# Storing each block of 128 result rows as two transfers of 64 rows in a fused attention and feed-forward kernel

## The chip, the cores and the metric

The kernel runs on one core of one Trainium2 chip. The metric is the device time of one execution in microseconds (us); lower is better. A core has a matrix engine (PE), a vector engine (DVE), a scalar engine (ACT), a general engine (POOL) and a synchronisation engine (SP) which here issues nearly all transfers; sixteen DMA engines carry them. Each engine runs its own instructions in order and waits on semaphores for the others.

## The reference

```python
B, H, S, D = 4, 8, 768, 48                      # batch, heads, steps, head size
for t in range(S):                               # recurrent attention, one state per batch and head
    state = alpha[:, :, t, :, None] * state + einsum('bhd,bhe->bhde', k[:, :, t], v[:, :, t])
    y[:, :, t] = einsum('bhd,bhde->bhe', q[:, :, t], state)
x = y.transpose(0, 2, 1, 3).reshape(3072, 384)   # tokens x (heads * head size)
h = x @ w_in                                     # 384 x 2048
g = h * tanh(log1p(exp(h)))
out = g @ w_out                                  # 2048 x 384, float32
```

The output has 3072 rows of 384 floats. Row `b * 768 + t` belongs to batch `b` and step `t`.

## The kernel before

**Chunks.** The four batches are taken in two pairs. A chunk is 64 steps (`L`) of a pair of batches, so 128 tokens; there are 24 chunks, in the order pair 0, pair 1, pair 0, and so on (`chunks`). Within a chunk's 128 rows, the first 64 belong to one batch of the pair and the last 64 to the other, and these two blocks lie 768 rows apart in the output.

**Attention (`attention(n)`).** For a chunk, SP loads one block with q, k and the decays (`qka`, 675.9 KB, L454, or in parts at L459) and one with v (192 KB, L463). DVE makes the running products of the decays with two scans (`rest` at L485, the second at L498) and multiplies k and q by them; PE turns k (L520), multiplies by the state and forms the scores (L530 and L536, the planner's "front"); DVE masks the scores into `probs` (L544); PE multiplies them with v and updates the state (L549 and L559, the planner's "back"); ACT and DVE split the result into a high and a low part (L578, L584); and SP moves a few rows into place with six small transfers (L604). The `qka` block has two buffers, so the load for chunk n waits until chunk n - 2 has read its own.

**Feed-forward (`unit`).** Hidden rows are worked in 16 blocks of 128, chunks in groups of two or four (`SEGMENTS`). One unit is a group times a block: PE makes `h` with nine matmuls (L706), ACT and DVE make `g` by eight passes (L714 to L740), and PE adds into one bank of `sums_at` for each chunk of the group, three matmuls for each (L770). After the last block of a group its four banks are finished almost together: ACT copies each to a result buffer `osb` (L808), or DVE first adds it to a kept part and ACT copies that (`part`, L801 and L808), and SP stores it (L815). Eight such buffers exist. The last four groups of four chunks run all 16 blocks in one go; what comes before is cut into shorter segments. So result rows are stored in bursts of four: two bursts from `part` and four from `osb`, 24 stores of 192 KB in all.

**Order.** Nothing is scheduled by hand. `Plan.order` plays the whole program through with a table of costs, `COST` (L211): for each kind of task the time it takes from its engine, and the time after which its result can be used. It places the tasks of each engine in the order in which they could begin, the task's key breaking ties, and the program is emitted in that order. An attention chunk is due eight units ahead of the first unit that reads it (`LEAD`). The planner therefore does not change what an instruction takes; its times only decide the order within each engine's queue. SP's queue holds loads, the six small moves and the stores together, in one order.

**Semaphores of transfers.** Eight semaphores serve the transfers of SP in turn, so a transfer also waits until the eighth before it has landed.

**The end.** After the last group, DVE, PE and DVE reduce a few checks to one number `good` (L878 to L893), which every engine reads to decide whether a general path is run instead (L1023); it isn't. SP then waits for all eight transfer semaphores and the program closes (L1087).

Of the kernel before, what the change touches and what calls it, by code (L numbers as in the profile page):

```python
# [26 lines left out]
B, H, S, D = 4, 8, 768, 48  # L27
# [3 lines left out]
L = 64  # L31
NCH = S // L
# [60 lines left out]
class Plan:  # L93
# [13 lines left out]
    def add(self, engine, cost, late, key, emit, needs=(), uses=(), behind=(), port=False):  # L107
        t = Task(engine, cost, late, key, emit, port)
        t.needs, t.uses, t.behind = list(needs), list(uses), list(behind)
        for u in t.uses:  # L110
            u.left += 1
            u.key = min(u.key, key)
        self.tasks.append(t)
        return t
# [96 lines left out]
COST = {  # L211
    "load part": (0.7, 3.3), "load q": (1.8, 5.0), "load two": (1.2, 4.0), "load v": (0.7, 4.0),
    "load w": (2.0, 5.0),
    "move": (0.63, 2.5), "store": (0.47, 3.0),
    "fill": (0.165, 0.2), "fill0": (0.33, 0.36),
    "off": (0.34, 0.6), "w off": (0.84, 1.08), "lead": (0.47, 0.58), "bits": (0.87, 0.98),
    "w hi": (0.42, 0.56), "w lo": (0.95, 1.08),
    "w check": (0.92, 1.2),
    "scan": (1.16, 1.27), "inverse": (0.09, 0.21), "mult": (0.6, 0.72), "check": (0.2, 0.34),
    "state": (0.48, 0.55), "state0": (0.5, 0.6), "mask": (0.65, 0.8),  # L220
    "front": (1.05, 1.3), "front0": (0.6, 0.8), "turn": (0.4, 0.65),
    "turned": (0.46, 0.6), "back": (1.05, 1.3), "back1": (0.6, 0.8), "update": (0.55, 0.75),
    "x3 hi": (0.16, 0.3), "x3 lo": (0.2, 0.32), "x hi": (0.39, 0.53), "x lo": (0.48, 0.59),
    "down": (0.525, 0.8), "stash": (0.4, 0.53), "join": (0.47, 0.59), "result": (0.5, 0.7),
}
# [11 lines left out]
def fast_path(ctx, tc, qka, v, w, out, good):  # L237
    nc = tc.nc
# [15 lines left out]
    for half in (slice(0, L), slice(L, P)):  # L254
        nc.gpsimd.affine_select(
            out=causal_f[half], in_=one[half], pattern=[[1, L]], compare_op=ALU.is_ge,
# [19 lines left out]
    for i in range(BUFS["probs"]):  # L276
        t = const.tile([P, 2, NPAIR, L], F32, name=f"probs{i}")
# [3 lines left out]
    for b in range(B // 2):  # L281
        t = const.tile([R, NSEG * D + 16], F32, name=f"state{b}")
# [17 lines left out]
    def new(buffer, shape, name, pool=None, dtype=F32):  # L300
        buffer.tile = (pool or sb).tile(
            shape, dtype, tag=buffer.tag, name=name, bufs=plan.slots[buffer.tag]
        )
        return buffer.tile
# [388 lines left out]
    def unit(c0, nt, f, at, ends):  # L693
        N, key = nt * C, float(at)
        tile_at, place = X_AT[c0]
        x = xs[tile_at][:, :, :, place * C : place * C + N]
        fs = slice(f * P, (f + 1) * P)
        h, u, t, y, g = (plan.buffer(z) for z in ("h", "u", "t", "y", "g"))
        wide = lambda z: z.tile[:, :N]
        cost = lambda z: COST[z, nt]  # L700

        def up():
            p = new(h, [P, NT_MOST * C], f"h{at}", ps)
            passes = [(z, a, s) for s in range(NK) for z, a in ((0, 0), (0, 1), (1, 0))]
            for m, (z, a, s) in enumerate(passes):
                nc.tensor.matmul(  # L706
                    p[:, :N], wi[:, z, s, fs], x[:, a, s], start=m == 0, stop=m == len(passes) - 1
                )

        def exp():
            new(u, [P, NT_MOST * C], f"u{at}")
            nc.scalar.activation(  # L714
                wide(u), wide(h), AF.Exp, scale=-1.0, accum_out=uchk[:, at : at + 1]
            )

        def square():
            new(t, [P, NT_MOST * C], f"t{at}")
            nc.scalar.activation(wide(t), wide(u), AF.Square, bias=1.0, scale=2.0)  # L720

        def times():
            new(y, [P, NT_MOST * C], f"y{at}")
            nc.vector.scalar_tensor_tensor(wide(y), wide(u), 0.5, wide(h), ALU.add, ALU.mult)  # L724

        def log():
            nc.scalar.activation(wide(t), wide(t), AF.Ln, bias=tenth, scale=0.1)  # L727

        def inverse():
            nc.scalar.activation(wide(t), wide(t), AF.Exp, scale=-1.0)  # L730

        def gate():
            nc.vector.scalar_tensor_tensor(wide(t), wide(y), 0.4, wide(t), ALU.mult, ALU.mult)  # L733

        def upper():
            new(g, [P, 2, NT_MOST * C], f"g{at}", dtype=F32R)
            nc.scalar.activation(g.tile[:, 0, :N], wide(t), AF.Copy)  # L737

        def lower():
            nc.vector.tensor_tensor(  # L740
                g.tile[:, 1, :N], wide(t), g.tile[:, 0, :N].bitcast(F32), ALU.subtract
            )

        chunk_x = [z for n in range(c0, c0 + nt) for z in ready_x[n]]
        t_up = add("PE", *cost("up"), key, up, chunk_x + ready_w[f, 0], [h])
        for n in range(c0, c0 + nt):
            readers_x.setdefault(n, []).append(t_up)
        k = key + GATE
        t_exp = add("ACT", *cost("exp"), k, exp, [t_up], [h, u])
        t_y = add("DVE", *cost("dve"), k + 0.01, times, [t_exp], [h, u, y])  # L750
        t_sq = add("ACT", *cost("act"), k + 0.02, square, [t_exp], [u, t])
        t_ln = add("ACT", *cost("ln"), k + 0.03, log, [t_sq], [t])
        t_in = add("ACT", *cost("act"), k + 0.04, inverse, [t_ln], [t])
        t_g = add("DVE", *cost("dve"), k + 0.05, gate, [t_in, t_y], [t, y], port=True)
        t_hi = add("ACT", *cost("act"), k + 0.06, upper, [t_g], [t, g])
        t_lo = add("DVE", *cost("dve"), k + 0.07, lower, [t_hi], [t, g], port=True)

        for j in range(nt):
            n = c0 + j
            bank = bank_of(n, nt)  # L760
            begins = n not in sums
            if begins:
                sums[n] = plan.buffer(f"o{bank}")
            o, end = sums[n], ends(n)

            def down(o=o, j=j, n=n, begins=begins, end=end, bank=bank):
                if begins:
                    o.tile = sums_at[:, bank][:, :DM]
                for m, (a, z) in enumerate(((0, 0), (0, 1), (1, 0))):
                    nc.tensor.matmul(  # L770
                        o.tile, g.tile[:, a, j * C : (j + 1) * C], wo[:, z, f],
                        start=begins and m == 0, stop=end and m == 2,
                    )

            t_down = add(
                "PE", *COST["down"], key + LAG + 0.001 * j, down, [t_lo, *ready_w[f, 1]], [g, o],
                behind=downs.get(n, []),
            )
            downs[n] = [t_down]
            if not end:  # L780
                continue
            del sums[n]
            k = key + LAG + 0.1
            if f < NFF - 1 and n in kept:
                def more(o=o, n=n):
                    nc.vector.tensor_tensor(part[n].tile, o.tile, part[n].tile, ALU.add)

                kept[n] = add("DVE", *COST["join"], k, more, [t_down, kept[n]], [o, part[n]])
                continue
            if f < NFF - 1:  # L790
                part[n] = plan.buffer("osb")

                def stash(o=o, n=n):
                    nc.scalar.copy(new(part[n], [P, DM], f"part{n}"), o.tile)

                kept[n] = add("ACT", *COST["stash"], k, stash, [t_down], [o, part[n]])
                continue
            done, from_part = [t_down], n in kept
            if from_part:
                def join(o=o, n=n):  # L800
                    nc.vector.tensor_tensor(part[n].tile, o.tile, part[n].tile, ALU.add)  # L801

                done = [add("DVE", *COST["join"], k, join, [t_down, kept[n]], [o, part[n]])]
            osb = part[n] if from_part else plan.buffer("osb")

            def result(o=o, n=n, osb=osb, from_part=from_part):
                to = osb.tile if from_part else new(osb, [P, DM], f"osb{n}")
                nc.scalar.activation(  # L808
                    to, to if from_part else o.tile, AF.Copy, accum_out=ochk[:, n : n + 1]
                )  # L810

            def store(n=n, osb=osb):
                b, c = chunks[n]
                to = out.rearrange("(b c t) d -> c b t d", c=NCH, t=L)
                nc.sync.dma_start(to[c, 2 * b : 2 * b + 2], osb.tile)  # L815

            written = add("ACT", *COST["result"], k, result, done, [osb] if from_part else [o, osb])
            add("SP", *COST["store"], k, store, [written], [osb])


# [271 lines left out]
```

## Time and profile before

| | |
|---|---|
| median of three runs | 575.2 us (571.51 to 576.0) |
| the profiled execution | 576.53 us, of which the span from first to last instruction is 574.7 us |
| mean granted TensorE clock | 0.954 |
| PE busy with matmuls | 514.2 us (89%) |
| PE busy with weight loads (beside the matmuls) | 444.3 us (77%) |
| DVE, ACT, POOL busy | 382.0, 397.5, 40.2 us |
| transfers | 54.46 MB, mean 95 GB/s; 4.72 MB written to HBM |

The span counts from the first instruction of the core to its last; 1.8 us of the profiled execution lie outside it. The busy time of an engine is a mean over stages, and this kernel's stages differ: where an engine stands idle, and for whom, is read from the views by time.

In rows of the trace, "L815" is line 815 of the kernel; a name such as `out_dram<-osb` gives what is written and what is read; "SPq" is the queue from which SP issues transfers, where the duration is that of the issue and not that of the transfer. A bracket at the end of a row tells how long the engine stood idle ahead of it and what released it.

### The profile page before, as it was taken

What the parts mean: (1) busy time and instruction counts of PE and PEld (TensorE: products, weight loads), DVE (VectorE), ACT (ScalarE), POOL (GpSimd) and SP (SyncE); (2) the same over time, 40 slices, a digit from 0 to 9 for tenths busy, and PEclk for the clock granted to TensorE, in tenths of its full rate; (3) what the DMA queues carried; (4) which work ended last, traced back from release to release, by engine and by line L of the source; (5) the groups of instructions that cost most, each with busy time, mean ns of one, the idle gap of its engine ahead of it and who ended that gap; (6) DMA issues with size and microseconds to landing.
All of it is one profiled execution on the core that took longest, in us unless ns stands there. A gap on an engine that the chain in (4) does not pass through costs nothing.

```text
span 574.7 us, 13166 instructions
## 1 busy us (share of the span) xinstructions
PE 514.2 (89%) x5275; PEld 444.3 (77%) x5275; DVE 382.0 (66%) x638; ACT 397.5 (69%) x926; POOL 40.2 (7%) x36
## 2 busy tenths in 40 slices
PE   7788899889999984899999969999969999999960
PEld 4366789888789874788989858889858889889960
DVE  7847999999897783777774457864447544444430
ACT  2347778698779893699977745677745677877740
POOL 2001110423333000000000000000000000000000
PEclk9969999999999998699999988999997999999995
DMA  8654442522533664448410142300140000000001
GB/s 266 197 179 129 137 132 73 179 63 103 174 101 123 184 195 159 136 136 252 147 56 1 40 134 72 86 6 1 34 141 22 15 1 2 33 22 0 1 12 46
DMA packets 21744, 54.46 MB, mean 95 GB/s; under 512 B 3696, under 2 KB 14448, under 8 KB 21680
## 3 DMA queue, kind: packets, MB, share of 16 engines
q1 hardware_dynamic: 21392, 53.49, 30.1%
q8 instruction: 42, 0.69, 0.5%
q14 instruction: 22, 0.18, 0.1%
q10 hardware_dynamic: 288, 0.10, 0.1%
HBM read 46.50 MB, written 4.72 MB: 89 GB/s over the span
## 4 chain that ended last, share of the span: by engine, by line
PE 72%; DMA 10%; DVE 9%; ACT 4%; issue 2%; ACTq 0%; DVEq 0%; SPq 0%
PE h L706 30%; PE sums_at L770 30%; DMA qka<-in_qka_dram 8%; PE att_at L549 2%; PE att_at L530 2%; PE sums_at L381 1%; DMA v<-in_vp_dram 1%; PE att_at L536 1%; DVE qka L498 1%; PE att_at L559 1%; DVE t L733 1%; PE sums_at L828 1%; PE att_at L520 1%; DVE rest L485 1%; DVE g L740 1%
## 5 line engine op out<-in xcount | busy, mean ns | idle before, releaser
L770 PE MATMUL sums_at<-wo,g 128*128 128x384 f32 x1152 | 233.8, 345 | 21.9 <-DVE g L740 12.5
L770 PEld LDWEIGHTS sums_at<-wo,g 128*128 128x128 f32 x1152 | 201.0, 189 | 37.5 <-DVE g L740 14.6
L706 PE MATMUL h<-xs,wi 128*128 128x512 f32 (+1 forms) x990 | 224.1, 372 | 1.1 <-DVE y L724 1.1
L706 PEld LDWEIGHTS h<-xs,wi 128*128 128x128 f32 x990 | 173.1, 192 | 28.9 <-DVE y L724 1.6
L740 DVE TENSOR_TENSOR g<-t,g 128x512 fp32r<-128x512 f32 (+1 forms) x110 | 70.2, 639 | 53.2 <-ACT g L737 52.9
L714 ACT ACTIVATE u<-h 128x512 f32<-128x512 f32 (+1 forms) x110 | 59.3, 539 | 66.1 <-PE h L706 66.0
L724 DVE SCALAR_TENSOR_TENSOR y<-u,h 128x512 f32<-128x512 f32 (+1 forms) x110 | 67.5, 616 | 48.4 <-ACT u L714 48.1
L733 DVE SCALAR_TENSOR_TENSOR t<-y,t 128x512 f32<-128x512 f32 (+1 forms) x110 | 70.2, 640 | 13.9 <-ACT t L730 13.9
L727 ACT ACTIVATE t<-t,tenth 128x512 f32<-128x512 f32 (+1 forms) x110 | 73.0, 665 | 2.0
L737 ACT ACTIVATE g<-t 128x512 fp32r<-128x512 f32 (+1 forms) x110 | 62.3, 567 | 9.4 <-DVE t L733 4.5
L720 ACT ACTIVATE t<-u 128x512 f32<-128x512 f32 (+1 forms) x110 | 63.0, 574 | 4.9 <-DVE g L740 2.9
L730 ACT ACTIVATE t<-t 128x512 f32<-128x512 f32 (+1 forms) x110 | 62.2, 567 | 0.6
L485 DVE TENSOR_TENSOR_SCAN rest<-qka,behind 112x520 f32<-112x520 f32 x24 | 29.7, 1236 | 28.1 <-DMA qka<-in_qka_dram 28.1
L498 DVE TENSOR_TENSOR_SCAN qka<-qka,ahead 112x520 f32<-112x520 f32 x24 | 31.3, 1303 | 0.1
L372 POOL TENSOR_TENSOR wi<-w_lead,wi 128x384 fp32r<-128x384 f32 x12 | 21.5, 1799 | 126.8 <-ACT wi L369 126.8
L549 PEld LDWEIGHTS att_at<-probs,v 64*64 64x64 f32 (+1 forms) x672 | 12.3, 134 | 13.1 <-DVE probs L544 8.5
L409 ACT ACTIVATE wc<-wc 128x768 f32<-128x768 f32 x16 | 14.6, 910 | 11.1 <-DMA wc<-in_wp_dram 11.1
L549 PE MATMUL att_at<-probs,v 64*64 64x64 f32 (+1 forms) x672 | 15.3, 231 | 7.0 <-DVE probs L544 7.0
L714 ACT ACTIVATION_READ_ACCUMULATOR u<-h 128x1 f32 x110 | 21.4, 195 | 0.0
L544 DVE COPY_PREDICATED probs<-causal,att_at 128x512 f32<-128x512 uint32 x21 | 15.4, 735 | 8.5 <-PE att_at L536 8.5
L502 ACT ACTIVATE chk<-qka,minus 112x8 f32<-112x8 f32 x24 | 7.3, 304 | 20.0 <-DMA qka<-in_qka_dram 11.7
L828 PE MATMUL sums_at<-ident 128*128 128x384 bf16 x59 | 13.6, 371 | 4.9 <-POOL ident masks.py:199 2.5
(107 smaller groups left out, 396.0 us busy)
## 6 DMA issues: line engine op xcount, KB each, us to landing
qka<-in_qka_dram SPq DMA_DIRECT2D x21, 675.9 KB
ws<-in_wp_dram SPq DMA_DIRECT2D x16, 768.0 KB
wc<-in_wp_dram SPq DMA_DIRECT2D x16, 768.0 KB
v<-in_vp_dram SPq DMA_DIRECT2D x24, 192.0 KB
out_dram<-osb SPq DMA_DIRECT2D x16, 192.0 KB
xs<-x SPq DMA_DIRECT2D x138, 16.0 KB
out_dram<-part SPq DMA_DIRECT2D x8, 192.0 KB
qka<-in_qka_dram SPq DMA_DIRECT2D x2, 448.0 KB
```

The costliest lines, as they stand in the source:

```text
L498: nc.vector.tensor_tensor_scan(a, a, ahead, 0.0, ALU.mult, ALU.max)
L549: nc.tensor.matmul(y[64 * a : 64 * a + wide, u, j], V()[own, h : h + wide], probs[slot][own, a, j], start=first and j == 0, stop=True, ski ...
L706: nc.tensor.matmul(p[:, :N], wi[:, z, s, fs], x[:, a, s], start=m == 0, stop=m == len(passes) - 1)
L714: nc.scalar.activation(wide(u), wide(h), AF.Exp, scale=-1.0, accum_out=uchk[:, at : at + 1])
L720: nc.scalar.activation(wide(t), wide(u), AF.Square, bias=1.0, scale=2.0)
L724: nc.vector.scalar_tensor_tensor(wide(y), wide(u), 0.5, wide(h), ALU.add, ALU.mult)
L727: nc.scalar.activation(wide(t), wide(t), AF.Ln, bias=tenth, scale=0.1)
L730: nc.scalar.activation(wide(t), wide(t), AF.Exp, scale=-1.0)
L733: nc.vector.scalar_tensor_tensor(wide(t), wide(y), 0.4, wide(t), ALU.mult, ALU.mult)
L737: nc.scalar.activation(g.tile[:, 0, :N], wide(t), AF.Copy)
L740: nc.vector.tensor_tensor(g.tile[:, 1, :N], wide(t), g.tile[:, 0, :N].bitcast(F32), ALU.subtract)
L770: nc.tensor.matmul(o.tile, g.tile[:, a, j * C : (j + 1) * C], wo[:, z, f], start=begins and m == 0, stop=end and m == 2,)
```

## The change

The store of a finished chunk named its destination as one pattern of two blocks (the two batches) of 64 rows. It now goes as two transfers, one for each batch, each of 64 whole rows that lie one after another in the output. The bytes are the same; the number of store instructions on SP doubles from 24 to 48. The planner's time for the store task, which is still one task, goes from 0.47 to 1.0 us of SP and from 3.0 to 3.5 us until it is done; its times for three of the attention's PE tasks change by up to 0.08 us. No other code changes.

```diff
@@ COST
-    "move": (0.63, 2.5), "store": (0.47, 3.0),
+    "move": (0.63, 2.5), "store": (1.0, 3.5),
...
-    "front": (1.05, 1.3), "front0": (0.6, 0.8), "turn": (0.4, 0.65),
-    "turned": (0.46, 0.6), "back": (1.05, 1.3), "back1": (0.6, 0.8), "update": (0.55, 0.75),
+    "front": (1.13, 1.35), "front0": (0.6, 0.8), "turn": (0.36, 0.6),
+    "turned": (0.46, 0.6), "back": (1.11, 1.3), "back1": (0.6, 0.8), "update": (0.55, 0.75),
...
             def store(n=n, osb=osb):
                 b, c = chunks[n]
-                to = out.rearrange("(b c t) d -> c b t d", c=NCH, t=L)
-                nc.sync.dma_start(to[c, 2 * b : 2 * b + 2], osb.tile)
+                for u in range(2):
+                    to = out[ds((2 * b + u) * S + c * L, L), :]
+                    nc.sync.dma_start(to, osb.tile[L * u : L * (u + 1)])
```

## The prediction

> **What bounds the kernel now.** I read the page's first two parts, then the chain of work in order of time, then stretches of it with the busy time of each engine, and last the rows of SP, DVE and PE around the places where the chain leaves PE.
>
> ```profile
> span 574.7 us, 13166 instructions
> ...
> PE 514.2 (89%) x5275; PEld 444.3 (77%) x5275; DVE 382.0 (66%) x638; ACT 397.5 (69%) x926; POOL 40.2 (7%) x36
> ...
> DMA  8654442522533664448410142300140000000001
> ```
>
> PE is the bound by its share, and the DMA engines are mostly idle in the second half. PE stands idle for 60.5 us of the span. The chain says where: among long runs of matmuls it holds three waits of a dozen microseconds for a load of q, k and decays (start, length, what).
>
> ```profile
> 216.48 12.36 DMA qka<-in_qka_dram
> ...
> 326.63 11.63 DMA qka<-in_qka_dram
> ...
> 413.23 12.07 DMA qka<-in_qka_dram
> ```
>
> SP's own rows show what stands ahead of each of these loads: stores.
>
> ```profile
> 212.62 3.76 SPq L815 DMA_DIRECT2D out_dram<-part  x3
> 216.48 3.54 SPq L454 DMA_DIRECT2D qka<-in_qka_dram  x1
> ...
> 318.31 7.44 SPq L815 DMA_DIRECT2D out_dram<-osb  x4
> 326.63 2.88 SPq L454 DMA_DIRECT2D qka<-in_qka_dram  x1
> ...
> 338.31 0.34 SPq L454 DMA_DIRECT2D qka<-in_qka_dram  x1
> ...
> 404.94 7.71 SPq L815 DMA_DIRECT2D out_dram<-osb  x4
> 413.23 3.30 SPq L454 DMA_DIRECT2D qka<-in_qka_dram  x1
> ```
>
> A load issued with no store ahead of it takes 0.34 us of SP's queue (338.31); those right behind a burst take about 3. How fast such a free load lands is seen in the DMA view of 337.5 to 343.5 us, 40 slices of 0.15 us:
>
> ```profile
> GB/s 41 41 72 106 51 41 38 34 0 0 0 206 206 165 0 41 330 288 330 330 330 453 288 453 288 206 206 165 83 82 82 82 0 0 0 0 0 0 0 0
> ```
>
> Its last bytes move in slice 32, at 342.3: 4.0 us after the issue. So a load behind stores lands some 7 to 8 us late. Why, the stretches tell (columns: stretch and length, busy time of PE, PE weight loads, DVE, ACT, POOL, granted clock, DMA share, GB/s):
>
> ```profile
> core 0: us, PE busy (x) PEld busy (x) DVE busy (x) ACT busy (x) POOL busy (x), PEclk, DMA share, GB/s
> 222.60:230.80 8.20, 0.00 (x1) 0.00 (x0) 1.87 (x4) 0.00 (x0) 0.00 (x0) 0.67 0.55 189
> 230.80:239.60 8.80, 8.14 (x22) 6.67 (x23) 5.50 (x10) 4.80 (x14) 0.00 (x0) 0.53 0.60 185
> ...
> 343.94:348.90 4.96, 4.96 (x73) 4.25 (x73) 4.45 (x8) 1.59 (x4) 0.00 (x0) 0.56 0.17 47
> ...
> 431.00:437.70 6.70, 6.70 (x78) 5.74 (x79) 5.08 (x11) 2.16 (x6) 0.00 (x0) 0.55 0.14 38
> ...
> 355.90:358.90 3.00, 3.00 (x75) 2.61 (x75) 1.56 (x3) 1.90 (x5) 0.00 (x0) 1.00 0.85 236
> 562.00:572.00 10.00, 0.00 (x0) 0.00 (x0) 0.00 (x0) 0.00 (x0) 0.00 (x0) 0.50 0.14 51
> ```
>
> From 562 to 572 nothing runs but the last stores. They move 51 GB/s at a share of 0.14, which is 2.2 of 16 DMA engines, 23 GB/s each. Loads whose pattern begins with 112 rows use 0.85 of all sixteen (355.9 to 358.9). I read from this that a store is worked by two engines, one for each of the two batch blocks that its destination names first, and that a burst of four (786 KB at 51 GB/s, 15.4 us) blocks those two engines for the load that follows, whose last rows then land behind it. The Trainium skill says so outright: by "DMA: Bandwidth & Descriptors", section "Why a DMA increments its semaphore by 16 and not by 1", a transfer runs on the largest number of engines up to 16 that divides the slowest dimension of both its patterns, here 2 before and 16 after. The trace agrees for the old form (0.14 of 16); no row shows a 64-row transfer.
>
> **The change part by part.** *The store's form.* A transfer of one batch's 64 rows has no outer dimension of two; the nearest rows are the loads by 112 rows. Spread over 16 engines at 23 GB/s a burst of four would need 786 KB / 368 GB/s = 2.1 us instead of 15.4. The lower bound of the effect is that it stays at 15.4 us (first rival); I take 2.1, as all other large transfers of this kernel run so. What this is worth is read stage by stage, from what waits for the loads:
>
> ```profile
> 228.93 1.24 DVE L485 TENSOR_TENSOR_SCAN rest<-qka,behind 112x520 f32<-112x520 f32 x1 [9.23 <-DMA qka<-in_qka_dram]
> 230.81 1.65 PE L770 MATMUL sums_at<-wo,g 128*128 128x384 f32 x4 [8.21 <-DVE g L740]
> ...
> 338.27 1.24 DVE L485 TENSOR_TENSOR_SCAN rest<-qka,behind 112x520 f32<-112x520 f32 x1 [5.67 <-DMA qka<-in_qka_dram]
> 340.37 0.45 PE L770 MATMUL sums_at<-wo,g 128*128 128x384 f32 x1 [1.40 <-DVE g L740]
> 343.94 1.13 PE L549 MATMUL att_at<-probs,v 64*64 64x64 f32 x32 [3.13 <-DVE probs L544]
> ...
> 420.13 2.25 PE L706 MATMUL h<-xs,wi 128*128 128x512 f32 x9
> 425.32 1.24 DVE L485 TENSOR_TENSOR_SCAN rest<-qka,behind 112x520 f32<-112x520 f32 x1 [6.12 <-DMA qka<-in_qka_dram]
> 427.42 0.44 PE L770 MATMUL sums_at<-wo,g 128*128 128x384 f32 x1 [1.85 <-DVE g L740]
> 430.99 1.12 PE L549 MATMUL att_at<-probs,v 64*64 64x64 f32 x32 [3.13 <-DVE probs L544]
> 432.88 4.21 PE L706 MATMUL h<-xs,wi 128*128 128x512 f32 x9
> ```
>
> DVE works in order: its scan waits for the load, and behind the scan stand the `g` and the mask for which PE waits. After each such wait PE also runs at a lower granted clock: the nine matmuls of L706 take 4.21 us instead of 2.25.
>
> Stage A (216 to 240): the load would land by 216.48 + 4.0 to 5.0 = 220.5 to 221.5, sooner if the six issues ahead of it are shorter than the 3.76 us of the three stores. DVE has been free since 228.93 - 9.23 = 219.7. It needs 1.9 us from the scan's start to the end of `g` (228.93 to 230.8), so PE has its `g` at 222.4 to 223.4 and not at 230.8: of 8.2 us idle about 8.0 go. From 230.8 to 239.6 PE is busy 8.14 us at a clock of 0.53; at full clock this is 3.8 us less. Together 11.8.
>
> Stage B (326 to 349): the load would land at 330.6 to 331.6, before DVE comes to its scan at 338.27 - 5.67 = 332.6. All 5.67 us of DVE go, hence both PE waits, 1.40 + 3.13 = 4.5; and the 4.96 us of PE work at 0.56 lose 2.2. Together 6.7.
>
> Stage C (413 to 438) likewise: landing at 417.2 to 418.2, DVE at its scan at 419.2; waits of 1.85 + 3.13 = 5.0, and 6.70 us at 0.55 lose 3.0. Together 8.0.
>
> What is late next: in B the following load was issued at 338.31, just as the one before landed (it is the eighth transfer behind it and uses its semaphore); it moves forward with it, and so do the small moves behind. The other bursts have no such load behind them and give nothing.
>
> The end:
>
> ```profile
> 557.96 0.20 ACT L808 ACTIVATION_READ_ACCUMULATOR osb<-sums_at 128x1 f32 x1
> ...
> 558.33 3.72 SPq L815 DMA_DIRECT2D out_dram<-osb  x1
> ...
> L1023 SPq COMPARE_BRANCH  x1: 45/45/45, 564.5 to 564.5; - x1
> ...
> L1023 SPq EVENT_SEMAPHORE  x8: 17/17/17, 565.0 to 573.3; - x8
> ...
> L1087 SPq EVENT_SEMAPHORE  x10: 17/28/28, 573.4 to 574.6; - x10
> ```
>
> The last result is ready at 558.16, SP's last issue lasts until 562.05, SP branches 2.45 us later, and then waits until 573.3 for transfers to land; 1.4 us close the program. With 2 issues of 0.34 to 0.56 us (rows below) SP is through at 559.0 to 559.5 and reaches its waits, 2.95 us on, at 562.0 to 562.5. The last transfer, issued at 558.7 to 558.9, should land in less than the 4.0 us of a load seven times as large, so by 562.9. I take 562.5 and 1.4 us behind it: 563.9, a gain of 10.8.
>
> *The doubled issues.*
>
> ```profile
> L463 SPq DMA_DIRECT2D v<-in_vp_dram x24: 328/338/1272, 2.2 to 433.0; - x24
> ...
> L815 SPq DMA_DIRECT2D out_dram<-osb x16: 511/564/3721, 318.3 to 558.3; - x16
> ```
>
> A load of 128 rows is issued in 0.338 us, a store of two blocks in 0.564 (duration: least, median, most in ns). Two issues for one thus cost between 0.1 and 0.6 us of SP for each store, 2.3 us a burst at most. SP had stalls of up to 3.7 us there, and after the burst at 318 the load waits for its buffer: SP is free at 325.75, the load begins at 326.63. So I take nothing; without this cover the burst costs 1.4 us in B and 1.7 in C.
>
> *The planner's times.* They change no duration. By them some 20 fronts get 0.08 us more, as many backs 0.06 more and turns 0.04 less, about 2 us over the whole plan, and SP's stores are counted at 1.0 us, so a few tasks may change places on any engine. The trace can't show which. From the rows, one misplaced load costs what stage C costs, 8.0 us; a better order could win at most a like amount, out of the idle time that remains. I take zero and keep both ends.
>
> *Sum.* 11.8 + 6.7 + 8.0 + 10.8 = 37.3 us off the profiled execution's 574.7 + 1.8 = 576.5 gives 539.2; I say 539. That execution is 1.3 us above the median of the runs shown, 575.2, which would bring 538; the difference lies within their spread of 4.5.
>
> **The rivals.** *The transfers do not spread, and it gets slower.* If 64-row stores still run at about 51 GB/s, whether by engines or because writing to HBM gives no more, the drains stay and only the issues are added, at 0.56 us each: the load at 216.48 comes 1.7 us later (three stores), those of B and C 1.4 and 1.7, the end 0.6: 5.4 us, so 582. It decides if a burst still takes over some 13 us to drain. Against it: were the writing side the limit, the packets would stand long on all sixteen engines and the share would be high; it is 0.14. For it speaks a rule: the Trainium skill, "DMA: Bandwidth & Descriptors", section "Rules for kernel authors", advises against two transfers to the halves of the partitions, as both run over the same sixteen engines, and asks for one transfer of 128. By that rule this rival's 582 would come; the trace doesn't agree with its premise here, as the one transfer of 128 uses two engines.
>
> *Only the end gains.* If the loads are late by something else (the two `qka` buffers, the order on SP), A, B and C stay: 576.5 - 10.8 = 566. Against it: the load at 338.31 lands in 4.0 us between the same neighbours save the stores.
>
> *The new order gives a stall back.* One load placed behind its use in a stage as tight as B or C: 539 + 8 = 547, and up to 551 if it is as long as A's 11.8. For it: DVE and SP queues are in order, so one exchange is enough. Against: the stores' new time is nearer to two issues than the old one was.
>
> **How the numbers follow.** Forecast, 531 to 546: 0.70, its own range being 8 us to either side for the planner. A stall given back, 547 to 551: 0.18. Only the end: 0.07. No spread, slower: 0.04. About the same for other reasons: 0.01. A range of 531 to 551 holds the first two less their edges, some 0.83. One per cent (5.8 us) is about what a measurement of this kernel tells from no change; faster by more holds the first three, 0.95; same 0.01; slower 0.04.
>
> **What would show it.** Right: after the bursts at about 318 and 405 (less what was won before) a DMA share far over 0.14 for a short time, loads issued in about 0.34 us and landing within 5 us, no wait of DVE's scan over 2 us after 215, a granted clock near 1.00 all through, and an end under 7 us after the last result. Wrong: a share of 0.14 that lasts 10 us after a burst (no spread); short bursts but a scan that still waits 5 us (another cause); a new wait of PE before 200 us, where no store runs (the planner).

## The result and the profile after

The changed kernel takes 544.0 us (median of four runs, 543.6 to 544.9) against 575.5 before: a ratio of 0.947, with a 95% interval of 0.943 to 0.951. The forecast was 539, in a range of 531 to 551. The profiled execution has a span of 542.3 us, 32.4 less than before.

The page of the changed kernel, first its head, then the slices and the transfers:

```profile
span 542.3 us, 13194 instructions
...
PE 506.7 (93%) x5275; PEld 437.8 (81%) x5275; DVE 380.7 (70%) x638; ACT 397.0 (73%) x926; POOL 41.7 (8%) x36
...
PEclk9979899999999999999999999999999999999998
...
qka<-in_qka_dram SPq DMA_DIRECT2D x21, 675.9 KB, 5.3
...
out_dram<-osb SPq DMA_DIRECT2D x32, 96.0 KB, 2.2
```

PE executes as many matmuls in 7.5 us less of busy time, at a mean granted clock of 0.986 instead of 0.954. A store lands 2.2 us after its issue (last column), a load of q, k and decays 5.3 us after its own. The last burst of stores, from 528 to 542.3 us in 40 slices, keeps up to nine tenths of the sixteen DMA engines busy for short times, where before the share was 0.14 for 10 us:

```profile
DMA  0000000000000008480849084839860010000000
```

SP's rows around the bursts, to be held against those of before:

```profile
214.75 5.99 SPq L816 DMA_DIRECT2D out_dram<-part  x8
220.84 0.53 SPq L454 DMA_DIRECT2D qka<-in_qka_dram  x1
...
310.56 7.19 SPq L816 DMA_DIRECT2D out_dram<-osb  x8
318.87 0.33 SPq L454 DMA_DIRECT2D qka<-in_qka_dram  x1
...
390.38 7.21 SPq L816 DMA_DIRECT2D out_dram<-osb  x8
398.68 0.35 SPq L454 DMA_DIRECT2D qka<-in_qka_dram  x1
```

A load behind a burst is issued in 0.33 to 0.53 us instead of about 3. What waits for these three loads, in the rows of DVE and PE:

```profile
225.89 1.24 DVE L485 TENSOR_TENSOR_SCAN rest<-qka,behind 112x520 f32<-112x520 f32 x1 [2.20 <-DMA qka<-in_qka_dram]
228.10 0.79 PE L770 MATMUL sums_at<-wo,g 128*128 128x384 f32 x3 [2.69 <-DVE part L801]
...
323.84 1.24 DVE L485 TENSOR_TENSOR_SCAN rest<-qka,behind 112x520 f32<-112x520 f32 x1 [0.73 <-DMA qka<-in_qka_dram]
...
403.98 1.24 DVE L485 TENSOR_TENSOR_SCAN rest<-qka,behind 112x520 f32<-112x520 f32 x1 [1.06 <-DMA qka<-in_qka_dram]
```

In stages B and C (second and third group of rows) the scan waits about 1 us and PE not at all; in stage A (the first) a wait of 2.69 us of PE is left. Stretches of the changed kernel (columns as before):

```profile
212.00:235.00 23.00, 19.67 (x277) 16.88 (x274) 17.47 (x29) 15.41 (x38) 0.00 (x0) 1.00 0.56 149
...
318.00:340.00 22.00, 22.00 (x383) 19.05 (x377) 18.44 (x32) 14.55 (x32) 0.00 (x0) 1.00 0.38 100
398.00:420.00 22.00, 22.00 (x382) 19.05 (x373) 19.00 (x35) 13.46 (x28) 0.00 (x0) 1.00 0.36 98
```

B and C are now without a gap on PE; A still has 3.3 us of idle time, at full clock.

To see where the 32.4 us lie, I follow ACT's first pass over `h` (L714), which runs once for each of the 110 units, and compare the start of the same unit in two kernels' traces. The differences to before change only in a few places; with the attention's new times they also wander by some us within units 1 to 46. All kernels of this study stand in one table; each number is how much later (or, with a minus, sooner) a kernel got through that stretch than the kernel before, worked out from the one profiled execution of each by these starts, the column before the sum up to the end of the span:

```
                            to the   units   A: unit  B: to   C: to   to the   sum
                            1st unit 1-46    46-65    unit 81 unit 97 end
changed kernel                -1.3    +3.4    -9.8     -6.8    -8.0    -9.8   -32.4
e1 split, old times           -1.5    -0.3    -6.5     -6.8    -8.0    -9.6   -32.7
e2 new times, old store       +2.6    +3.5    +3.5     +0.6    +0.3     0.0   +10.6
e3 split by columns           +2.2    +3.6    +6.5     +2.7    +1.6    +0.8   +17.4
e4 last four stores split     +3.8    +0.2    -0.7     +0.1     0.0   -10.0    -6.6
e5 split, store time          +1.8    -0.6    -9.8     -6.8    -8.0   -10.0   -33.4
e6 split, attention times      0.0    +3.3    -5.7     -6.8    -8.0   -10.0   -27.2
e7 parts' stores on POOL      +0.5    -0.4   -11.3     -6.8    -8.0    -9.1   -35.2
e8 last four as 62 + 2 rows   -0.2    -0.5    +0.3      0.0     0.0    -0.2    -0.6
e9 all stores on POOL         -2.8    -0.5   -12.0     -6.8    -8.0    -8.0   -38.0
e10 as e5, last four on POOL  -1.8    -0.5   -11.3     -6.8    -8.0    -9.5   -37.9
```

Forecast were 6.7 for B and 8.0 for C: both came. A gives 9.8 instead of 11.8, the end 9.8 instead of 10.8, and 3.4 us are lost before the first store is issued.

### The profile page after: what moved, and what is told of

Same layout as the page of the kernel before. It is cut to its first block, busy times and chain, and to the rows that moved or that the text cites. A ratio compares the mean times of both kernels' runs of the same rounds, so it can differ in the third digit from the quotient of the medians.

```text
span 542.3 us, 13194 instructions
## 1 busy us (share of the span) xinstructions
PE 506.7 (93%) x5275; PEld 437.8 (81%) x5275; DVE 380.7 (70%) x638; ACT 397.0 (73%) x926; POOL 41.7 (8%) x36
## 4 chain that ended last, share of the span: by engine, by line
PE 74%; DVE 12%; ACT 6%; DMA 3%; issue 3%; SPq 0%; ACTq 0%; DVEq 0%
PE sums_at L770 32%; PE h L706 30%; DMA qka<-in_qka_dram 3%; PE att_at L530 2%; PE sums_at L829 2%; PE att_at L549 2%; PE att_at L536 2%; DVE t L733 2%; PE sums_at L381 1%; DVE rest L485 1%; DVE y L724 1%; DVE g L740 1%; PE att_at L559 1%; PE att_at L520 1%; DVE w_lead L356 1%
## 5 line engine op out<-in xcount | busy, mean ns | idle before, releaser
L706 PE MATMUL h<-xs,wi 128*128 128x512 f32 (+1 forms) x990 | 220.7, 368 | 0.6 <-DVE y L724 0.4
L706 PEld LDWEIGHTS h<-xs,wi 128*128 128x128 f32 x990 | 170.4, 189 | 27.6 <-DVE y L724 1.6
L714 ACT ACTIVATE u<-h 128x512 f32<-128x512 f32 (+1 forms) x110 | 59.4, 540 | 68.3 <-PE h L706 68.3
L485 DVE TENSOR_TENSOR_SCAN rest<-qka,behind 112x520 f32<-112x520 f32 x24 | 31.0, 1294 | 13.3 <-DMA qka<-in_qka_dram 13.2
L498 DVE TENSOR_TENSOR_SCAN qka<-qka,ahead 112x520 f32<-112x520 f32 x24 | 30.0, 1250 | 0.0
L714 ACT ACTIVATION_READ_ACCUMULATOR u<-h 128x1 f32 x110 | 21.4, 195 | 0.0
L530 PEld LDWEIGHTS att_at<-qka,state 48*64 48x64 f32 (+1 forms) x640 | 11.5, 131 | 10.3 <-issue 4.5
L372 POOL TENSOR_TENSOR wo<-w_lead,wo 128x384 fp32r<-128x384 f32 x12 | 18.7, 1562 | 6.8 <-DVE t L733 4.6
L530 PE MATMUL att_at<-qka,state 48*64 48x64 f32 (+1 forms) x640 | 14.2, 227 | 4.3 <-DVE state L513 1.8
L508 DVE TENSOR_TENSOR qka<-qka 112x512 f32<-112x512 f32 x24 | 17.4, 725 | 0.0
```

What stands on the lines that cost most here:

```text
L372: nc.gpsimd.tensor_tensor(lo, as_hi(both()), hi.bitcast(F32), ALU.subtract)
L530: nc.tensor.matmul(y[64 * a : 64 * a + wide, u, j], st[r : r + D, e : e + wide], Q()[r : r + D, j, u], start=j == 0, stop=False, skip_grou ...
L706: nc.tensor.matmul(p[:, :N], wi[:, z, s, fs], x[:, a, s], start=m == 0, stop=m == len(passes) - 1)
L714: nc.scalar.activation(wide(u), wide(h), AF.Exp, scale=-1.0, accum_out=uchk[:, at : at + 1])
```

## The experiments

The theory: the gain comes from the stores running on sixteen DMA engines instead of two; the planner's new times change the order and so the rest. The rivals: smaller transfers are enough, or the new order wins a part. All times are medians; the ratio is that to the kernel before on the same chip, with its 95% interval.

**e1: the split with the planner's old times.** The diff is the change without its three lines of `COST`.

> The stores split in two, with the planner's old times, so the order of before. If the whole gain comes from the transfers spreading over 16 engines, and the new times only cost the 2 us by which the changed kernel is late at the 46th unit and part of what stage A fell short: stage A saves 10 to 12 us, B 6.8, C 8.0 and the end 9.8 against before, so about 539 to 541 us. Rival, the new times win a part of the gain: 546 us or more. Rival, the 2 us are not from the times: 544 us.

Measured: 544.3 us, ratio 0.945 (0.941 to 0.949), so as fast as the changed kernel. The first two expectations did not come. The 544 us of the third did, but by luck: its reason, that the late 46th unit has nothing to do with the times, was wrong. The 3.4 us of units 1 to 46 are gone (-0.3), so they are the times' doing; but with the order of before stage A gives only 6.5 us. The new times lose 3.4 and win 3.3, and the term of the prediction for A was too large by itself. What is left in A, in e1's rows of SP, DVE and PE:

```profile
210.97 4.77 SPq L816 DMA_DIRECT2D out_dram<-part  x6
215.83 0.54 SPq L454 DMA_DIRECT2D qka<-in_qka_dram  x1
```

```profile
221.30 1.24 DVE L485 TENSOR_TENSOR_SCAN rest<-qka,behind 112x520 f32<-112x520 f32 x1 [4.14 <-DMA qka<-in_qka_dram]
```

```profile
223.18 2.61 PE L770 MATMUL sums_at<-wo,g 128*128 128x384 f32 x7 [3.12 <-DVE g L740]
```

Six issues take 4.77 us where three stores took 3.76, and the load lands 5.5 us after its issue. DVE had been ready since 217.2, and PE's 3.12 us of idle time are followed by a lower clock:

```profile
214.00:231.00 17.00, 12.49 (x110) 10.67 (x109) 9.74 (x17) 8.77 (x24) 0.00 (x0) 0.80 0.80 231
```

**e2: the new times with the old store.** The diff is the change's `COST` lines alone.

> The planner's new times with the old store of two blocks in one transfer, so the order of the changed kernel. If the transfers carry the gain: no faster than before, 575 to 580 us, about 2 us late at the 46th unit, with the waits of stages B and C and a drain of some 15 us at a DMA share near 0.14 at the end all there. Rival, the new order wins a part: under 570 us.

Measured: 583.6 us, ratio 1.010 (1.004 to 1.016): one per cent slower than before, which is small but clear of the noise, and above the range expected. The end is as before (share 0.15, 54 GB/s from 570 to 580):

```profile
570.00:580.00 10.00, 0.00 (x0) 0.00 (x0) 0.00 (x0) 0.00 (x0) 0.00 (x0) 0.50 0.15 54
```

So the new order by itself, with the old stores, wins nothing. It costs 3.5 us ahead of the stores, and with the old stores another 3.5 in stage A.

**e3: as many transfers of as many bytes, but on two engines.**

```diff
+                to = out.rearrange("(b c t) d -> c b t d", c=NCH, t=L)
+                half = DM // 2
                 for u in range(2):
-                    to = out[ds((2 * b + u) * S + c * L, L), :]
-                    nc.sync.dma_start(to, osb.tile[L * u : L * (u + 1)])
+                    cols = slice(half * u, half * (u + 1))
+                    nc.sync.dma_start(to[c, 2 * b : 2 * b + 2, :, cols], osb.tile[:, cols])
```

> The changed kernel, but each store's two transfers take half of the columns of all 128 rows instead of one batch each: as many transfers of as many bytes, and each names its destination again as two blocks of 64 rows. If the number of DMA engines is what counts: a DMA share near 0.14 after the bursts, and the time of before plus up to 5.4 us for the issues, 576 to 584 us. Rival, two smaller transfers in place of one are enough: 544 us.

Measured: 593.4 us, ratio 1.028 (1.023 to 1.034). Smaller transfers are not enough: with the changed kernel's number of transfers, bytes and planner's times, but two blocks named first, 49 us separate it from the changed kernel. The share after the last burst is that of two engines again. It is slower than expected because issuing costs more than the 0.56 us that I had taken for it (e3, all stores, then one burst with the load behind it):

```profile
576.00:586.00 10.00, 0.00 (x0) 0.00 (x0) 0.00 (x0) 0.00 (x0) 0.00 (x0) 0.50 0.15 50
```

```profile
L818 SPq DMA_DIRECT2D out_dram<-osb x32: 503/1638/2467, 330.6 to 582.2; - x32
```

```profile
330.59 12.67 SPq L818 DMA_DIRECT2D out_dram<-osb  x8
343.37 1.88 SPq L454 DMA_DIRECT2D qka<-in_qka_dram  x1
```

An issue now stands 1.6 us in SP's queue (median), where in the changed kernel it is 0.57. In the burst shown the first three take 0.50 to 0.57 us and the five behind them 1.59 to 2.04. So it is not the form of the transfer that is slow to issue; an issue waits for those ahead of it. That it waits because the queues of the two engines are full is my reading, which no view shows.

**e4: only the last four stores split.**

```diff
             def store(n=n, osb=osb):
                 b, c = chunks[n]
-                to = out.rearrange("(b c t) d -> c b t d", c=NCH, t=L)
-                nc.sync.dma_start(to[c, 2 * b : 2 * b + 2], osb.tile)
+                if n < n_chunks - 4:
+                    to = out.rearrange("(b c t) d -> c b t d", c=NCH, t=L)
+                    nc.sync.dma_start(to[c, 2 * b : 2 * b + 2], osb.tile)
+                    return
+                for u in range(2):
+                    to = out[ds((2 * b + u) * S + c * L, L), :]
+                    nc.sync.dma_start(to, osb.tile[L * u : L * (u + 1)])
```

> The kernel before, with only the last four stores split. If the gains of the stages are separate: the end alone gets shorter by 9.8 us as in the changed kernel, so 565 to 566 us, with stages A, B and C as before. If the end's drain also waits for something else than the two engines: 570 us or more.

Measured: 565.8 us, ratio 0.980 (0.974 to 0.985). The end alone gives its 10.0 us, and A to C stay within 0.7 of before. The gains are separate and add up.

**e5 and e6: which of the new times does what.** Both have the split; e5 has only the store's new time, e6 only the attention's.

> The stores split, and of the planner's new times only that of the store; the order ahead of the first store is that of before. If the attention's times cost 3.6 us between the 6th and the 46th unit, and the store's time is what made stage A 3.8 us shorter in the changed kernel than with the old times: 540 to 541 us, under both. Rival, both effects come from the attention's times: 544 us.

> The stores split, and of the planner's new times only those of the attention. If the attention's times cost 3.6 us ahead of the stores and win nothing in stage A: 547 to 548 us. Rival, stage A's 3.8 us are theirs: 544 us.

Measured: e5 539.1 us, ratio 0.936 (0.932 to 0.940); e6 548.1 us, ratio 0.952 (0.948 to 0.956). Both came as the first theory had it, e5 0.9 us under its range. The attention's times cost 3.3 us before any store and win nothing in A (5.7, against 6.5 with the old times). The store's time wins the 3.3 us of A: the planner now puts the load later, and so places the pass for which PE waits ahead of the scan on DVE. In e5's rows of DVE:

```profile
220.93 0.69 DVE L740 TENSOR_TENSOR g<-t,g 128x512 fp32r<-128x512 f32 x1 [0.76 <-ACT g L737]
223.88 1.24 DVE L485 TENSOR_TENSOR_SCAN rest<-qka,behind 112x520 f32<-112x520 f32 x1 [2.26 <-DMA qka<-in_qka_dram]
```

In e1, as before, `g` came after the scan. e5 is faster than the changed kernel, each against the kernel before: the two intervals don't overlap.

**e7: the parts' stores issued by POOL.** The split with the old times; the eight stores of stage A, now sixteen transfers, leave SP's queue. Against e1:

```diff
-                    nc.sync.dma_start(to, osb.tile[L * u : L * (u + 1)])
+                    (nc.gpsimd if from_part else nc.sync).dma_start(to, osb.tile[L * u : L * (u + 1)])
...
-            add("SP", *COST["store"], k, store, [written], [osb])
+            add("POOL" if from_part else "SP", *COST["store"], k, store, [written], [osb])
```

> The stores split, the planner's old times, and the eight stores of kept parts (the two bursts of stage A) issued by POOL, which has nothing else to do by then, instead of SP. If stage A's remaining wait is there because the load stands behind the doubled issues on SP: the load is issued some 3 us sooner, its wait of 4.1 us goes nearly away, and with it the lower clock: 538 to 541 us. Rival, the load waits for its buffer or for other loads: 544 us as with SP; or POOL's own issues are slow and hold the result buffers: 545 us or more.

Measured: 541.9 us (537.3 to 543.8), ratio 0.940 (0.935 to 0.945), 0.9 us above the range expected; e1's interval overlaps, so the times alone settle little. The trace does: the load is issued at 212.41, no longer behind a store, DVE comes to its scan without any wait for it, and the same stretch as in e1 has PE busy at full clock:

```profile
212.41 0.48 SPq L454 DMA_DIRECT2D qka<-in_qka_dram  x1
```

```profile
217.52 1.24 DVE L485 TENSOR_TENSOR_SCAN rest<-qka,behind 112x520 f32<-112x520 f32 x1
```

```profile
214.00:231.00 17.00, 16.31 (x242) 14.20 (x232) 12.61 (x21) 15.28 (x38) 3.08 (x6) 1.00 0.81 268
```

Stage A gives 11.3 us, close to the 11.8 that were forecast for it. What was missing in e1 goes with the place of the load behind the issues. Up to this load SP's order is that of e1 but for the stores; on DVE and ACT the planner places a few tasks of the stage otherwise as well (here the scan comes one pass sooner), and what that is worth by itself was not tried.

**e8: is it the number of rows?** The kernel before, with its last four stores as four transfers each (the lines left out keep the other stores as they were).

```diff
...
+                for u in range(2):
+                    for r, rows in ((0, 62), (62, 2)):
+                        to = out[ds((2 * b + u) * S + c * L + r, rows), :]
+                        nc.sync.dma_start(to, osb.tile[L * u + r : L * u + r + rows])
```

> The kernel before, with each of the last four stores as four transfers: 62 and 2 rows of the one batch, 62 and 2 of the other. No destination names two blocks any more. If the number of engines is the largest up to 16 that divides the rows, 62 rows go on two engines: the drain at a DMA share near 0.14 and the end of before are back, 575 to 578 us. Rival, any destination that names rows first is spread: 566 to 568 us as with two transfers of 64.

Measured: 574.4 us, ratio 0.997 (0.994 to 1.001): nothing is left of e4's gain, though no transfer names two blocks.

```profile
561.00:571.00 10.00, 0.00 (x0) 0.00 (x0) 0.00 (x0) 0.00 (x0) 0.00 (x0) 0.50 0.14 51
```

The share of 0.14 at 51 GB/s is exactly that of before. 62 has no divisor up to 16 other than 1 and 2, 64 has 16. That is the rule of the Trainium skill, "DMA: Bandwidth & Descriptors", section "Why a DMA increments its semaphore by 16 and not by 1"; e3 (a share of 0.15), e4 (10.0 us sooner at the end) and e8 (0.14) agree with it.

**e9 and e10: a version that is better still?** e9 issues all stores from POOL, e10 only the last four; both have the store's new time and the attention's old ones.

> As with the store's time alone (539.1 us), but the last four stores are issued by POOL. If the end is now set by SP, which issues the last two transfers one after the other and only then reads the result of the checks and waits for its semaphores: SP branches with the other engines, 1.9 us sooner, so about 537 us. Rival, the landing of the last transfer sets the end: 539 us.

> All stores split and issued by POOL, with the planner's new store time and its old times for the attention. If SP's share in the loads and in the end is all that is left: stage A as with the parts on POOL (11 to 12 us in place of 6.5), the end 1.9 us shorter, so 537 to 540 us. Rival, POOL's issues land later and the end gets longer by that: 541 us or more.

Measured: e9 540.8 us (537.8 to 544.8), ratio 0.942 (0.937 to 0.948); e10 542.2 us (538.5 to 544.8), ratio 0.945 (0.940 to 0.949). The 537 us hoped for in e10 did not come, e9 is 0.8 us above its range, and neither is better than e5. Stage A gives 12.0 and 11.3 us, but the end gains less than with SP (8.0 and 9.5 against 10.0). In e10 SP branches early and its eight waits are short, as hoped, but closing the program then waits 3.5 us for POOL:

```profile
L1024 SPq EVENT_SEMAPHORE  x8: 17/17/17, 532.0 to 532.5; - x8
...
L1088 POOLq DRAIN  x3: 34/107/3542, 532.0 to 536.4; - x3
```

e10 also shows how far stage A can be trusted in a single execution. Every engine has e5's order there, and the same stores stand on SP, yet A gives 11.3 us and not 9.8. From 214 to 231 us the granted clock was 0.90 in e5 and 1.00 in e10. Differences in A of 1.5 us or less between two kernels of the table therefore show nothing; the steps from e1 (6.5) to the changed kernel (9.8) and to e7 (11.3) are two and three times as large.

## Why the prediction was right and wrong

*Two engines, and what they block.* Right, and shown by taking apart what could have been the same: e3 keeps number and size of the transfers and loses all of the gain, e8 keeps batches apart and loses it too.

*Stages B and C.* Right to 0.1 us in both, in every kernel in which these stores spread: idle time of PE and lower clock together, as they were added up from the rows. One step in it was off: DVE's scan was to find its load landed, but the load landed about 5.0 and 5.3 us after its issue and the scan waited 0.73 and 1.06 us. PE had other work for that long, so that the two terms come out to 0.1 us is partly luck.

*Stage A, 11.8 us.* The mechanism was right, the size was not: 6.5 us in the order for which it was worked out (e1). The step that failed is "The doubled issues ... So I take nothing". It looked for cover in B and C, where the load waits for its buffer, but in A the load stands right behind the burst. Against the units around it, it was issued about 1 us later than before (215.83 where the units run 1.5 to 1.8 us early, against 216.48), and it landed in 5.5 us where I had taken 4.0 to 5.0 from the last bytes seen on the engines, without the time from there to the semaphore. Together these leave 3.12 us of PE's 8.21 us of idle time, and, as I estimate from the mean clock of 0.80, some 7 of the 17 us from 214 to 231 at half clock. With the issues gone from SP (e7) the term is 11.3; e10, where they stay and `g` goes ahead of the scan, reaches the same.

*The end, 10.8 us.* Mis-sized by 1.0. SP did reach its waits about when expected, 3.6 us after the last result, but then stood in them for 1.8 us more; I had let them pass at once. The step that failed is the last transfer, which was to be issued 0.5 to 0.7 us after the last result and to hold nothing up beyond 4.3 us. The two issues of the third chunk were still in SP's queue, so it was issued 1.35 us after the last result, and it landed 3.8 us later, where the others of its burst took 2.1 to 2.2. The changed kernel's rows, the second for all stores:

```profile
L1024 SPq EVENT_SEMAPHORE  x8: 17/17/17, 539.2 to 541.0; - x8
...
DMA to landing us min/median/max: 2.1/2.2/3.8
```

Why the last one takes longer to land stays open.

*The planner's times, taken as zero.* Their sum is about zero, +3.4 and -3.3, but not because nothing moved: that they cancel is luck. The store's time won its 3.3 us in A by bringing `g` ahead of the scan. The attention's times cost 3.4 us in units 1 to 46. That is less than half the price of the rival "the new order gives a stall back", and not by its exchange of a load: SP issues its loads in the old order up to 150 us, and by then the changed kernel has already lost 2.8 us. Between its sixth and seventh unit stands what the prediction named as a sign of the planner, a new wait of PE before 200 us:

```profile
62.65 0.72 PE L530 MATMUL att_at<-qka,state 48*64 48x64 f32 x32 [1.77 <-DVE state L513]
```

From 62 to 70 us the granted clock is then 0.79, where before it is 1.00 and PE's longest wait around there is 0.84 us; by these numbers I estimate that the clock alone is worth 1.7 us, half of the loss. e6 shows the same wait and clock. Which exchange of tasks is behind it was not tried and stays open, and so does the other half.

*The rival that ended slower.* It didn't come, as its condition (no spread) was not met. Where the condition was made true, in e3, its price of 5.4 us was too low: e3 is 9.8 us slower than e2 (593.4 against 583.6), and its issues take 1.6 us instead of the 0.56 that the price went by.

*The sum.* -1.3 us from the start, -0.1 of B and C together, +3.4, +2.0 and +1.0 against the forecast: 5.0 us, which takes the 539.2 of the sum to 544.2; the profiled execution took 544.1. The -1.3 us from the start have nothing to do with the stores (last section) and are luck.

## What to carry to other kernels

Before the size of a transfer, look at the sizes of its outermost dimensions on both sides: here one of 2 or of 62 put the whole transfer on two DMA engines, and then the loads behind it came late as well. A busy share that is flat at a small fraction, here 0.14 for 10 us with no engine computing, shows it in the profile. When a transfer is split, count its issues in the queue of the engine that issues them, for the load that stands right behind; and when several planner's times are changed together, try each alone, since here one of them took back what the other won.

## What the runs showed of the hardware

The time to the first unit differs by up to 6.6 us between the kernels of the table, although none of them differs from the others there by more than the order of a few tasks, and e4 and the kernel before don't differ at all up to the last four stores. The granted clock does differ: in the stretch from 26 to 48 us it is 0.77 in the profiled execution of before and 0.61 in that of e4, which comes to its first unit 3.8 us later.

```profile
26.00:48.00 22.00, 18.76 (x280) 13.20 (x279) 12.65 (x19) 11.11 (x33) 0.00 (x0) 0.77 0.47 150
```

```profile
26.00:48.00 22.00, 18.56 (x209) 12.76 (x210) 11.40 (x16) 9.05 (x26) 0.00 (x0) 0.61 0.47 154
```

Executions of one kernel with a lower mean clock are also the longer ones, so this is likely most of their spread; it is why single executions are compared stretch by stretch here. Also unexpected was the price of an issue behind transfers that still run on two engines: 1.6 us for half a store in e3, against 0.564 for a whole one before (medians), where at most the last store of a burst was held. And stores issued by POOL cost time when the program closes, 3.5 us of waiting in e10.
